# RWKV-5 recurrence with a mixer MLP behind it, one core: w and u read into all partitions by DMA, the state decayed in place, 26 zero products, and order, buffers and engines laid out anew

## The chip, the core and the metric

The kernel runs on one core of one Trainium2 chip. A core has a matmul engine (TensorE, PE in the profile, with its weight loads as PEld), three engines for elementwise work (VectorE or DVE, ScalarE or ACT, GpSimd or POOL), and SyncE (SP), which here only issues DMAs. The engines run beside each other, each through its own list of instructions in order; semaphores hold an instruction until its inputs are there. The metric is the device time of one execution in microseconds; the time of a kernel is the median of its runs.

## What is computed

Batch 4, 8 heads, 768 steps, 48 features per head. For each batch and head a 48×48 state is carried through the steps, and then a token and a channel MLP follow:

```python
for t in range(S):
    kt, vt, rt = (k[:, :, t], v[:, :, t], r[:, :, t])
    cur = np.einsum('bhd,bhe->bhde', u[None] * kt, vt)
    y[:, :, t] = np.einsum('bhd,bhde->bhe', rt, state + cur)
    state = w[None, :, :, None] * state + np.einsum('bhd,bhe->bhde', kt, vt)
...
xt = x.transpose(0, 2, 1)
h = np.maximum(xt @ w_tok1, 0.0) @ w_tok2
u = x + h.transpose(0, 2, 1)
h2 = np.maximum(u @ w_ch1, 0.0) @ w_ch2
return (u + h2)
```

x is the output of the recurrence, of shape 4×768×384. All inputs and the output are float32; the kernel's matmuls are bf16 with sums in float32.

## The kernel before

**Chunks.** The 768 steps of a batch are cut into six chunks of 128 (`C` = 6), taken in pairs. Within a chunk, k and r are scaled by powers of w (tables `wnat`, `wpair`, `wp`, and for batch 0 two tables held in `u_sb` buffers), and turned so that features lie on partitions: by TensorE transposes (`tk_ps`, `tr_ps`, `trk`) for batches 0 and 1, by DMA transposes (`rk`) for batches 2 and 3. Scores k·r go to `at_ps`, VectorE multiplies them by a mask into `AT0` and `AT1`, and the outputs are `y_ps` = AT·v plus r times the state before the chunk. The step's own term u·k·r is summed per head (`ad_ps` from the products `pr`, or `rku` reduced) and multiplied by v (`yd`, `ydb`); for batch 0 TensorE adds it to `y_ps`. The result lands in `x_b`.

**The state.** `state()` (lines 604 to 652) sums k·v into the PSUM tile `kv_ps`, of 128 partitions by 384. Chunks are grouped: two to a group in batches 0 and 1, three in batches 2 and 3 (`GB`). Within a group the sums go on in one PSUM tile, and after each chunk a bf16 copy (`S_0` or `S_1`) is kept. At the end of a group VectorE multiplies the tile by the decay of the group (`wGm`) into a bf16 tile S (line 636), and the next group begins with a product of S by the identity, which puts the state back into PSUM (lines 619 to 621). Six groups have a successor, so there are six such products of 384 columns.

**The mixer.** For each batch `mixer()` makes the token MLP (`h_ps<-x_b`, `h1r`, `hx_ps` or `hT_ps`) and the channel MLP: 24 groups of `z_ps` (three products of 384 columns each), evacuated with a relu into `zr` by ScalarE or VectorE, and the second layer `h_ps<-wch,zr`. That is most of TensorE's work, and the recurrence of the next batch is laced into it.

**The start.** w and u come as single rows of 1.5 KB on ScalarE's DMA queue (lines 360 and 365); TensorE spreads each over all partitions by a product with a row of ones (`spread`, lines 439 to 444 and 496). ScalarE takes the logarithm of the spread w into `lnw` (line 447), and every table is an Exp of `lnw` times an index. Small loads bring w and u with heads on partitions (`w_heads`, `u_heads`) for the state's decay and for `u_blk` (lines 361 to 364), turned by the tiny products `wd_ps` and `ud_ps`. SP loads r, k and v of batch 0 into `zr` rooms. Until data are there TensorE multiplies zeros: `NWARM` = 20 units, 10 of one product of 512 columns, 10 of four products of 128 (lines 1191 to 1204).

**Order.** Nothing is scheduled by rules here: `ORDER` gives the order in which tasks are emitted, and so each engine's list; `ENGINES` says for each task that may go to two engines which one has it; `BUFS` gives every tile its buffer. Each SP request has to wait for the eighth before it.

## Time and profile before

| | |
|---|---|
| Time, median of 3 runs | 161.94 us (161.71, 161.94, 162.23) |
| Span of the profiled execution, first to last instruction | 160.1 us |
| Median over that span | 1.84 us |
| HBM read, written | 20.46 MB, 4.72 MB |
| DMA requests of SP (the hardware queue) | 23.40 MB, packets of 75.4% of 16 engines' span |
| Mean granted clock of TensorE | 0.997 |

The profiled execution is one of the kernel's executions; its own time is given as the span alone, and what lies around it is known only as the difference to the median of the runs.

How to read the profile. Times are us from the start of the span. In a list of groups a row says line, engine, operation, out<-in and shape, the count, then busy time and mean duration in ns, then the idle time before these instructions and what ended most of it. Nearly all instructions carry line 279 (279 is the helper through which they are emitted), so a row is known by its tiles. In a list in order of time a row has start, duration, engine, operation and tiles; several equal instructions may be merged ("x11", with the duration of all). A row ending in [1.07 <-DMA ...] waited 1.07 us for that. In the chain that ended last the rows are pieces with start and length. Matmuls overlap each other, so their mean duration is longer than their share of TensorE; the chain gives that share.

### The profile page before, as it was taken

How to read it: one execution, taken by the hardware profiler on the slowest of the kernel's cores; microseconds unless marked ns; L12 is line 12 of the kernel's file. 1: busy time of each engine (PE TensorE's matmuls, PEld its weight loads, DVE VectorE, ACT ScalarE, POOL GpSimd, SP SyncE). 2: the span in 40 equal slices, each digit the busy share in tenths (PEclk: the TensorE clock that was granted, in tenths of full speed). 3: DMA queues.
4: the chain of work that ended last, by engine and by line, in shares of the span. 5: the costliest groups of instructions: out<-in, count | busy, mean ns of one | idle time of the engine just before them, and what ended most of it. 6: DMA issues, size and time to landing. Idle time of an engine off the chain costs nothing.

```text
span 160.1 us, 4053 instructions
## 1 busy us (share of the span) xinstructions
PE 155.0 (97%) x1617; PEld 105.7 (66%) x1618; DVE 116.0 (72%) x237; ACT 67.1 (42%) x149; POOL 79.0 (49%) x103
## 2 busy tenths in 40 slices
PE   6999999999999999999999999999999999999991
PEld 3577766777666777666667766676677666666670
DVE  4669995437866998879969988997797455445432
ACT  2859774976332465442316614234353200522100
POOL 7328899417145498434999917398972000000000
PEclk9999999999999999999999999999999999999998
DMA  5999999999998995899999999999961051620142
GB/s 129 262 261 244 218 233 190 198 208 195 229 212 151 188 197 112 186 153 201 207 231 152 236 131 250 220 216 151 196 168 53 0 123 26 197 84 17 49 147 98
DMA packets 86821, 26.90 MB, mean 168 GB/s; under 512 B 81554, under 2 KB 85908, under 8 KB 86804
## 3 DMA queue, kind: packets, MB, share of 16 engines
q1 hardware_dynamic: 84448, 23.40, 75.4%
q0 software_dynamic: 2160, 3.15, 11.5%
q8 instruction: 12, 0.20, 0.6%
q10 hardware_dynamic: 196, 0.11, 0.2%
q14 instruction: 5, 0.04, 0.1%
HBM read 20.46 MB, written 4.72 MB: 157 GB/s over the span
## 4 chain that ended last, share of the span: by engine, by line
PE 95%; DVE 1%; ACT 1%; issue 0%
PE h_ps L279 36%; PE z_ps L279 30%; PE kv_ps L279 8%; PE y_ps L279 6%; PE at_ps L279 4%; PE hT_ps L279 3%; PE hx_ps L279 3%; PE tr_ps L279 1%; PE w_ps L279 1%; PE trk L279 1%; ACT ka L279 1%; ACT rkb L279 1%; PE tk_ps L279 1%; PE u_ps L279 1%; PE ad_ps L279 0%; DVE pr L279 0%
## 5 line engine op out<-in xcount | busy, mean ns | idle before, releaser
L279 PE MATMUL h_ps<-wch,zr 128*128 128x384 bf16 (+1 forms) x300 | 55.0, 320 | 0.0
L279 PE MATMUL z_ps<-uT,wch 128*128 128x384 bf16 x288 | 52.0, 327 | 0.0
L279 ACT ACTIVATE zr<-z_ps 128x384 bf16<-128x384 f32 x52 | 23.6, 490 | 50.9 <-PE z_ps L279 50.8
L279 PEld LDWEIGHTS <-wch 128*128 128x128 bf16 x288 | 32.0, 114 | 13.9 <-DVE x_b L279 0.4
L279 PEld LDWEIGHTS <-zr 128*128 128x128 bf16 x300 | 27.0, 97 | 14.7
L279 DVE TENSOR_SCALAR zr<-z_ps 128x384 bf16<-128x384 f32 x44 | 23.1, 551 | 15.3 <-PE z_ps L279 15.2
L279 DVE TENSOR_TENSOR AT<-at_ps,mask 128x512 bf16<-128x512 f32 x36 | 23.2, 680 | 1.5 <-PE at_ps L279 1.5
L279 POOL TENSOR_TENSOR yd<-vb,adg 128x384 f32<-128x384 bf16 x15 | 12.6, 847 | 9.1 <-DVE vb L279 3.8
L279 POOL TENSOR_TENSOR ku<-kt,u_bc 128x384 f32<-128x384 f32 x11 | 11.0, 1001 | 11.9 <-DMA kt<-in_k_dram 9.8
L279 POOL TENSOR_TENSOR kr<-kt,wnat 128x384 bf16<-128x384 f32 x13 | 13.3, 1025 | 1.1 <-PE z_ps L279 1.0
L279 PEld LDWEIGHTS <-kr 128*128 128x128 bf16 (+1 forms) x196 | 11.7, 97 | 3.1 <-issue 0.4
L279 POOL TENSOR_TENSOR kr<-rt,wp 128x384 bf16<-128x384 f32 x10 | 10.6, 1069 | 3.1 <-DMA rt<-in_r_dram 3.1
L279 POOL TENSOR_TENSOR rku<-ku,rt 128x384 f32<-128x384 f32 x9 | 9.3, 1028 | 5.2 <-DVE adg L279 4.7
L279 DVE TENSOR_TENSOR u_sb<-x_b,hT_ps 128x384 bf16<-128x384 bf16 x15 | 7.7, 551 | 5.2 <-PE hT_ps L279 5.0
L279 PEld LDWEIGHTS <-wtok 128*128 128x128 bf16 x78 | 7.2, 98 | 4.9 <-issue 0.6
L279 DVE TENSOR_TENSOR osb<-u_sb,h_ps 128x384 f32<-128x384 bf16 (+1 forms) x16 | 8.3, 523 | 3.0 <-PE h_ps L279 2.7
L279 DVE TENSOR_TENSOR x_b<-y_ps,yd 128x384 bf16<-128x384 f32 x18 | 9.7, 552 | 0.7 <-PE y_ps L279 0.6
L279 PE MATMUL kv_ps<-warm 128*128 128x128 bf16 (+1 forms) x49 | 8.2, 328 | 1.4 <-DVE warm L279 1.4
L279 PE MATMUL h_ps<-x_b,wtok 128*128 128x384 bf16 x48 | 8.8, 327 | 0.0
L279 ACT CAST S<-kv_ps 48x192 bf16<-48x192 f32 x20 | 6.2, 312 | 4.9 <-PE kv_ps L279 3.7
L279 PE MATMUL y_ps<-vb,AT 128*128 128x48 bf16 (+1 forms) x240 | 8.2, 182 | 0.0
L279 PEld LDWEIGHTS <-warm 128*128 128x128 bf16 x50 | 4.5, 125 | 4.9 <-issue 3.3
(106 smaller groups left out, 202.9 us busy)
## 6 DMA issues: line engine op xcount, KB each, us to landing
out_dram<-osb SPq DMA_DIRECT2D x23, 192.0 KB, 2.2
vt<-in_v_dram SPq DMA_DIRECT2D x18, 192.0 KB, 4.2
kt<-in_k_dram SPq DMA_DIRECT2D x18, 192.0 KB, 4.9
rt<-in_r_dram SPq DMA_DIRECT2D x12, 192.0 KB, 3.4
wch<-in_moe_w_ch_dram POOLq DMA_DIRECT2D x4, 384.0 KB, 7.1
zr<-in_k_dram SPq DMA_DIRECT2D x3, 384.0 KB, 6.1
zr<-in_r_dram SPq DMA_DIRECT2D x3, 384.0 KB, 5.8
zr<-in_v_dram SPq DMA_DIRECT2D x3, 384.0 KB, 6.4
```

What stands on the lines that cost most here:

```text
L279: return lambda *args, **kw: tc.keep_in_program_order(f(*args, **kw))
```

## The change

The new kernel computes the same. What differs:

- **w and u.** SP reads the row of w into all 128 partitions of `lnw` (128 rows of 1.5 KB, 192 KB), and Ln is taken in place. The same way u goes to `u_bc`, by a later request on SP. The row loads on ScalarE's queue, the row of ones, both spreads and the copy to `u_bc` are gone. The small loads of `w_heads` and `u_heads` and the table load of ScalarE no longer wait for the row of w.
- **State.** The sums of a batch stay in one PSUM tile for all its chunks. At the end of a group VectorE multiplies the tile by `wGm` in place, and a copy to bf16 by ScalarE or VectorE gives S. The identity products are gone.
- **Zero products.** 26 units instead of 20: 14 of 512 columns and 12 of four times 128.
- **Tables of r.** A second set for groups of two exists only if a batch with DMA transposes had such groups; here none has, so only two index columns are added.
- **Order, buffers, engines.** `ORDER`, `BUFS` and `ENGINES` are new throughout.

```diff
-NWARM = 20
-WIDE_AT = [
-    0, 1, 2, 3, 4, 5, 6, 7, 8, 9,
-]
+NWARM = 26
+WIDE_AT = list(range(14))
...
-    t_wrow = once("ACT", "dma_tiny", lambda: act.dma_start(w_row, row(w).unsqueeze(0)))
+    t_wrow = once("SP", "load_w", lambda: sp.dma_start(lnw, row(w).unsqueeze(0).to_broadcast([128, dm])))
...
-    t_urow = once("ACT", "dma_tiny2", lambda: act.dma_start(u_row, row(u).unsqueeze(0)), [t_wrow])
-    t_tab = once("ACT", "act_table", lambda: act.preload_act_table_set("natural_log_exp_and_others"), [t_wrow])
-    t_ones = once("DVE", "memset_s", lambda: dve.memset(ones, 1.0))
+    t_ubc = once("SP", "load_u", lambda: sp.dma_start(u_bc, row(u).unsqueeze(0).to_broadcast([128, dm])))
+    t_tab = once("ACT", "act_table", lambda: act.preload_act_table_set("natural_log_exp_and_others"))
...
-    t_wbc = once("PE", "spread", spread("w", w_row), [t_wrow, t_ones], take=("m",))
-    t_lnw = once("ACT", "act384", lambda: act.activation(lnw, U["w"], Ln), [t_wbc, t_tab], use=[(t_wbc, "m")])
+    t_lnw = once("ACT", "act384", lambda: act.activation(lnw, lnw, Ln), [t_wrow, t_tab])
...
         def add_state():
-            if g == 0:
+            if c == 0:
                 new_bank(f"kv{plan.buf('kv')}")
...
-            if g == 0:
-                if c > 0:
-                    pe.matmul(kv[0].rearrange("p a q d -> p (a q d)"), ident,
-                              states[b, c - 1].rearrange("p a q d -> p (a q d)"),
-                              start=True, stop=False, skip_group_check=True)
             products(kv[0])
...
                 new = sb("S0", [128, HP, 2, D], bf16)
-                dve.tensor_mul(new, kv[0], wGm[G])
+                copy(on, new, kv[0])
...
         else:
-            t_state[b, c] = add("DVE", "x384p", lambda: keep_state("DVE"), [t_k, t_wGm[G]], take=(Sn,), use=okv)
+            t_r = add("DVE", "x384p", lambda: dve.tensor_mul(kv[0], kv[0], wGm[G]), [t_k, t_wGm[G]], use=okv)
+            t_state[b, c] = flex(EITHER, keep_state, [t_r], take=("S0",), use=okv)
```

**SP's list at the start of the program**, before (zr are the rooms of batch 0, vt, kt and win the loads of batch 1):

```order
L279 DMA zr<-in_k_dram 128x8x96
L279 DMA zr<-in_r_dram 128x8x96 x2
L279 DMA zr<-in_k_dram 128x8x96 x2
L279 DMA zr<-in_r_dram 128x8x96
L279 DMA zr<-in_v_dram 128x8x96 x2
L279 DMA vt<-in_v_dram 128x8x48
L279 DMA zr<-in_v_dram 128x8x96
```

and in the changed kernel:

```order
L278 DMA zr<-in_r_dram 128x8x96
L278 DMA lnw<-in_w_dram 128x384
L278 DMA zr<-in_k_dram 128x8x96
L278 DMA zr<-in_r_dram 128x8x96
L278 DMA zr<-in_k_dram 128x8x96 x2
L278 DMA zr<-in_v_dram 128x8x96
L278 DMA zr<-in_r_dram 128x8x96
L278 DMA zr<-in_v_dram 128x8x96 x2
```

The first r now stands ahead of the first k, w between them, and the last r of the batch behind the first v.

**ScalarE's list at the start**, before (wp holds the small loads, wpair and u_sb are tables, rkb and ka the evacuated transposes):

```order
L279 DMA wp<-in_w_dram 1x384
L279 DMA wp<-in_w_dram 8x2x48
L279 DMA wp<-in_u_dram 8x2x48
L279 ACT_TABLE_LOAD
L279 ACTIVATE lnw<-w_ps 128x384
L279 DMA wp<-in_u_dram 1x384
L279 ACTIVATE wpair<-lnw,iota 128x384
L279 ACTIVATE u_sb<-lnw,iota 128x384 x2
L279 ACTIVATE wpair<-lnw,iota 128x384
L279 ACTIVATE lnwd<-wd_ps 64x4 x2
L279 ACTIVATE wG_88<-lnwd 128x4
L279 COPY ka<-tk_ps 128x1024
```

and in the changed kernel:

```order
L278 DMA wp<-in_u_dram 8x2x48
L278 DMA wp<-in_w_dram 8x2x48
L278 ACT_TABLE_LOAD
L278 ACTIVATE lnwd<-wd_ps 64x4 x2
L278 ACTIVATE wG_87<-lnwd 128x4
L278 ACTIVATE lnw<-lnw 128x384
L278 ACTIVATE wpair<-lnw,iota 128x384
L278 ACTIVATE wG_88<-lnwd 128x4
L278 ACTIVATE wpair<-lnw,iota 128x384
L278 ACTIVATE u_sb<-lnw,iota 128x384 x2
L278 COPY rkb<-tr_ps 128x1024
```

The small operations on `wd_ps` moved ahead of Ln, the tables of r ahead of those of k, and r's evacuation ahead of k's.

**VectorE's list in the later half of batch 0**, before (AT are masked scores, pr the products for u, S_0 the state inside a group, S the state at its end):

```order
L279 TENSOR_TENSOR S_0_93<-kv_ps,bm 128x384
L279 TENSOR_TENSOR AT_434<-at_ps,u_sb 128x512
L279 TENSOR_TENSOR pr_488<-tr_ps,ka 128x1024
L279 TENSOR_TENSOR S_495<-kv_ps,wGm_91 128x384
L279 TENSOR_TENSOR AT_510<-at_ps,u_sb 128x512
L279 TENSOR_TENSOR AT_524<-at_ps,u_sb 128x512
L279 TENSOR_TENSOR AT_554<-at_ps,u_sb 128x512
L279 TENSOR_TENSOR AT_584<-at_ps,u_sb 128x512
L279 TENSOR_TENSOR S_632<-kv_ps,wGm_91 128x384
```

and in the changed kernel:

```order
L278 TENSOR_TENSOR AT_407<-at_ps,u_sb 128x512
L278 TENSOR_TENSOR kv_ps<-kv_ps,wGm_90 128x384
L278 TENSOR_TENSOR AT_488<-at_ps,u_sb 128x512
L278 COPY adg_512<-ad_ps 128x16
L278 TENSOR_TENSOR AT_518<-at_ps,u_sb 128x512
L278 TENSOR_TENSOR S_0_92<-kv_ps,bm 128x384
L278 TENSOR_TENSOR pr_528<-tr_ps,ka 128x1024
L278 TENSOR_TENSOR AT_551<-at_ps,u_sb 128x512
L278 TENSOR_TENSOR kv_ps<-kv_ps,wGm_90 128x384
```

The group's decay is now written back into `kv_ps`; the copies of it (`S_494` and `S_605`) stand on ScalarE's list. The first of the two decays stands earlier, ahead of the third `pr`.

More of the change, by code (lines that the diff above doesn't have):

```diff
@@ L322 @@
     krs = [const.tile([128, 2, H, P], bf16, name=f"kr{i}") for i in range(NKP)]
-    ones = const.tile([1, 128], f32, name="ones")
     u_bc = const.tile([128, dm], f32, name="u_bc")
@@ L326 @@
     NW = C // 2
[L327 to L328 removed]
+    iota_i = const.tile([128, 4 + 2 + 2 * NG + 2], i32, name="iota_i")
+    iota = const.tile([128, 4 + 2 + 2 * NG + 2], f32, name="iota")
     ident_f = const.tile([128, 128], f32, name="ident_f")
@@ L495 @@
     t_ublk = once("DVE", "u_blk", make_ublk, [t_ud, t_ub0], use=[(t_ud, "m")])
-    t_us = once("PE", "spread", spread("u", u_row), [t_urow, t_ones], take=("m",))
-    t_ubc = once("ACT", "act384", lambda: act.copy(u_bc, U["u"]), [t_us], use=[(t_us, "m")])
-    t_wp = [decay(wp, g, 6 + NG + g, [t_io, t_wbc, t_us, t_wd, t_ud, t_uw]) for g in range(NG)]
+    TABLES = sorted({GB[n // C] for n in range(B * C) if STYLE[n][0] == "dma"})
+    wps = {3: wp}
+    t_wp = {3: [decay(wp, g, 6 + NG + g, [t_io, t_wd, t_ud, t_uw]) for g in range(NG)]}
+    if 2 in TABLES:
+        wps[2] = const.tile([128, 2, dm], f32, name="wnatr")
+        t_wp[2] = [decay(wps[2], g, 6 + 2 * NG + g, [t_io]) for g in range(2)]
     loaded, asked, sent = {}, {}, {}
     t_load, i_load = {}, {}
-    def wide(b):
-        return STYLE[b * C][0] in ("f32", "win")
     def two_steps(b, c, i):
-        return STYLE[b * C][0] == "win" or i == 1 and wide(b)
+        return STYLE[b * C + c][0] == "win" or i == 1 and STYLE[b * C + c][0] == "f32"
     def load(b, c, i):
```

142 lines of the change are left out of this document (64 added, 78 removed), and 119 rows, old and new, of tables (BUFS, ENGINES, ORDER).

## The prediction

> **What bounds the kernel now.** I read the page first: the span, the busy shares, the forty slices and the shares of the chain that ended last.
>
> ```profile
> span 160.1 us, 4053 instructions
> ...
> PE 155.0 (97%) x1617; PEld 105.7 (66%) x1618; DVE 116.0 (72%) x237; ACT 67.1 (42%) x149; POOL 79.0 (49%) x103
> ...
> PE   6999999999999999999999999999999999999991
> ...
> DMA  5999999999998995899999999999961051620142
> ...
> PE 95%; DVE 1%; ACT 1%; issue 0%
> ```
>
> TensorE is full from the second slice to the last but one, and the chain lies on it for 95%. But zero products count as busy, so the next view is the busy time by stage (PE, PEld, DVE, ACT, POOL, granted clock, DMA share, GB/s).
>
> ```profile
> 12.00:25.00 13.00, 12.67 (x304) 9.27 (x302) 12.76 (x24) 10.87 (x23) 11.45 (x15) 1.00 1.20 224
> 25.00:60.00 35.00, 35.00 (x399) 25.02 (x397) 23.64 (x51) 18.46 (x42) 18.26 (x21) 1.00 1.11 198
> 60.00:100.00 40.00, 40.00 (x411) 27.22 (x410) 34.91 (x68) 16.36 (x40) 27.50 (x29) 1.00 1.08 186
> ```
>
> From 12 to 25 us VectorE works 12.76 of 13.00 us, while TensorE still fills holes with zero products: there VectorE sets the pace. From 25 us on TensorE has no hole. So a microsecond of matmuls taken out after 25 us is a microsecond off the end, if its inputs keep up; before that, what counts is when VectorE begins its masks and how many operations it has. The third view is the order of time at the start.
>
> ```profile
> 0.81 0.46 SPq L279 DMA_DIRECT2D zr<-in_k_dram  x1
> 1.33 1.74 SPq L279 DMA_DIRECT2D zr<-in_r_dram  x2
> ...
> 2.78 1.64 PE L279 MATMUL w_ps<-wp,ones 1*128 1x384 f32 x2
> ...
> 4.46 0.49 ACT L279 ACTIVATE lnw<-w_ps 128x384 f32<-128x384 f32 x1 [0.31 <-PE w_ps L279]
> ...
> 4.98 0.62 ACT L279 ACTIVATE wpair<-lnw,iota 128x384 f32<-128x384 f32 x1
> ...
> 5.51 1.10 ACT L279 ACTIVATE u_sb<-lnw,iota 128x384 f32<-128x384 f32 x2
> ...
> 6.28 0.56 DVE L279 TENSOR_TENSOR kr<-zr,wpair 128x384 bf16<-128x384 f32 x1 [1.07 <-DMA zr<-in_r_dram]
> ...
> 6.62 0.57 PE L279 MATMUL wd_ps<-ident_f,wp 8*128 8x8 f32 x2
> ...
> 7.12 2.21 PE L279 MATMUL kv_ps<-warm 128*128 128x512 bf16 x11
> ...
> 9.17 0.61 PE L279 MATMUL tk_ps<-ident,kr 128*128 128x128 bf16 x8
> ...
> 9.82 1.01 ACT L279 COPY ka<-tk_ps 128x1024 bf16<-128x1024 bf16 x1 [2.00 <-PE tk_ps L279]
> ...
> 11.95 0.69 DVE L279 TENSOR_TENSOR pr<-tr_ps,ka 128x1024 bf16<-128x1024 bf16 x1 [1.49 <-ACT rkb L279]
> ```
>
> The last row begins the stretch that VectorE fills. It waits for two evacuations on ScalarE, which wait for two groups of transposes, which stand behind the zero products.
>
> **The change: w by the load queue.** w now comes second on SP's queue, behind one load of r. The prices are the rate of the loads at the start and the quickest landing of a request into zr:
>
> ```profile
> 5.00:6.00 1.00, 1.00 (x6) 0.58 (x5) 0.21 (x2) 1.00 (x2) 0.36 (x2) 1.00 1.26 263
> ...
> DMA to landing us min/median/max: 3.9/6.2/6.4
> ```
>
> The first request, of 384 KB, lands at 0.81+3.9 = 4.7; before, the second ended VectorE's wait at 6.28, some 1.5 later, which is 384 KB at 263 GB/s. So after: r at 4.7; w, 128 rows of 1.5 KB (192 KB), 0.75 later at 5.45; k at 6.95; r of the second window at 8.4; its k at 9.9. No row shows a load that reads one row of DRAM 128 times. Bounds for its landing after issue, from these rows:
>
> ```profile
> out_dram<-osb SPq DMA_DIRECT2D x23, 192.0 KB, 2.2
> ...
> win<-in_r_dram SPq DMA_DIRECT2D x3, 384.0 KB, 8.4
> ```
>
> Issued at about 1.3, w lands between 3.5 and 9.7. I take 5.45, by the rate, since the loads around it go at that rate. The Trainium skill ("DMA: Bandwidth & Descriptors", Latency and other measured facts) reports that streams in lock step at a row pitch of 4 MiB halved the rate, 207 to 103 GB/s, with channel aliasing as the inferred cause; one row read 128 times could be like that. By it w would land at 6.2, still before the point where lateness begins to cost (below), so the sum would stay and the slow rival come nearer. No run here shows it yet.
>
> Then ScalarE: Ln 0.49 to 5.95, first table 0.62 to 6.6, a small one and the second table to 7.4, two more (1.10) to 8.5. VectorE: the two r products at 6.6 and 7.4 (0.56 each), done at 8.0; the two k products follow their tables, done at 9.1; the second window's four run to 11.1. So the r transposes are ready at 8.0 and the k transposes at 9.1.
>
> **The zero products and the added wait.** Ahead of the first transposes stand 9 wide (512) and 24 narrow (128) zero products, where it was 7 and 24 and the w spread. 3 wide and 8 narrow took 2.2 (row at 7.12), so 9 and 24 take 6.6; with the two tiny products wd and ud, 0.57 and about 0.3, TensorE comes to the r transposes at 1.39+7.5 = 8.9, after the data. Twelve narrow ones lie between them and the k transposes: at the same pace about 1.0, so k's at 10.3, done 10.75; ScalarE's copy 1.01 gives 11.75. VectorE can start its long stretch at 11.8, against 11.95: **−0.15**. Two places hide lateness: 0.9 on TensorE (8.0 to 8.9) and 0.7 to 1.2 on VectorE's products, so w may land at 6.4 for nothing, and later each microsecond costs one.
> wd is now fourth in that row instead of seventh and waits for w's small load on ScalarE's queue, issued second. Queued behind it are zero products and the r transposes, and on ScalarE the Ln. Its landing lies between 2.8 (the first small load had landed when the spread of w began) and 6.6 (wd ran). I take 3.9, 0.3 after TensorE gets there; at 6.6 the start would slip by 3.0.
>
> **In-place decay.** These rows price it; the two kv rows are pieces of the chain without and with the identity product.
>
> ```profile
> L279 PE MATMUL kv_ps<-S,ident 128*128 128x384 bf16 x6 | 2.0, 329 | 0.0
> ...
> L279 DVE TENSOR_TENSOR S<-kv_ps,wGm 128x384 bf16<-128x384 f32 x6 | 3.3, 546 | 0.0
> ...
> L279 ACT CAST x_b<-y_ps 128x384 bf16<-128x384 f32 x4 | 1.9, 478 | 1.5 <-PE y_ps L279 1.5
> ...
> L279 DVE CAST vb<-vt 128x384 bf16<-128x384 f32 x3 | 1.0, 350 | 0.0
> ...
> L279 DVE TENSOR_TENSOR kr<-rt,wp 128x384 bf16<-128x384 f32 x2 | 1.9, 931 | 0.0
> ...
> 49.27 0.17 PE kv_ps L279 x4
> ...
> 54.76 0.33 PE kv_ps L279 x5
> ```
>
> Each identity product holds the chain for 0.33−0.17 = 0.16; six fall away. Two are in the start, where VectorE sets the pace, and count there for nothing; four come after 25 us: **−0.65**. VectorE keeps six multiplications, now from PSUM into PSUM; no row has that form, so between the cheapest and dearest rows of 384 elements, 0.35 and 0.93; I take the same 0.55. What is new is a copy behind each, 0.48 on ScalarE five times and on VectorE once, before the next kv product may start. Later this is hidden by the mixer's products that stand between; if one is not hidden it costs 0.55.
>
> **Order, buffers, engines.** On VectorE the stretch from the first `pr` to the last mask of batch 0 was 11.95 to 24.03:
>
> ```profile
> 12.55 0.35 DVE L279 CAST u_blk<-ud_ps 64x4 bf16<-64x4 f32 x2
> 12.93 0.79 DVE L279 TENSOR_TENSOR kr<-zr,u_sb 128x384 bf16<-128x384 f32 x1
> ...
> 22.16 1.87 DVE L279 TENSOR_TENSOR AT<-at_ps,u_sb 128x512 bf16<-128x512 f32 x3
> 23.99 0.68 DVE L279 TENSOR_TENSOR ydb<-vb,adg 128x384 bf16<-128x384 bf16 x1
> ```
>
> u_blk and one k product leave it (0.35+0.79 = 1.14); 12 masks, 3 `pr`, three state operations and one small copy stay. From 11.8 without a hole the last mask would end at 22.75. VectorE now waits for TensorE, which waits for ScalarE's copy of the state, twice; masks stand between (1.3 us against 0.48 and a kv product), and I charge 0.5 for what they don't cover: **−1.15+0.5 = −0.65**. The u spread and u_bc's copy leave the start and hide nothing else. Three identity products of x, 3×128 columns, stand ahead of the last outputs of batch 0 now; as many columns as one identity product of the state, taken out of what follows: **−0.16**. Later 15 of the 96 z evacuations pass from VectorE to ScalarE and GpSimd loses a net nine operations of about 1 us, most of them to VectorE; none of the three comes near its stage's length, so **0**.
>
> Sum: −0.15−0.65−0.65−0.16 = −1.6. Span 160.1−1.6 = 158.5. The runs' median is 161.94, 1.84 over the profiled span; with that around it: **160.3**. Own range 159.4 to 160.9 (0.5 of uncovered waits either way and the price of w within its cover).
>
> **Rivals.**
> The DMA sets the pace (161.3 to 162.7). The DMA row is 9s to slice 29. Both new loads add 384 KB: 0.75 at 263 GB/s and about 1.0 at the later 186. The chance of being late is at the scores of batches 2 and 3:
>
> ```profile
> 82.22 2.16 SPq L279 DMA_TRANSPOSE rk<-kr  x1
> ...
> 86.99 0.62 PE L279 MATMUL at_ps<-rk 48*128 48x128 bf16 x16
> ...
> rk<-kr SPq DMA_TRANSPOSE x12, 3.9
> ...
> 96.63 1.00 POOL L279 TENSOR_TENSOR ku<-kt,u_bc 128x384 f32<-128x384 f32 x1 [4.07 <-DMA kt<-in_k_dram]
> ...
> SPq L279 <- POOL kr L279: 9.6, 7, 4.9
> ```
>
> The scores came 4.8 after the issue, with 3.9 to land: 0.9 to spare. My forecast asks for them 1.6 sooner. If loads alone set the time, the gain is lost (161.9), and 1.75−0.9 comes on top (162.7). Against it: SP waited 9.6 us for GpSimd's products, so part of the lateness was GpSimd's, which loses nine of them.
>
> w comes late (slower). Place: Ln of w on ScalarE; price: 1 us for each us after 6.4; it cancels the gain at 8.0. At the landing of the slowest load, 9.7, the end is 160.3+3.3 = 163.6. For: no load of this form in the trace; against: rate and size.
>
> Half pace at the start. The rows give the clock as 1.00, yet 3 wide and 8 narrow products (2560 columns) took 2.2, 0.86 ns a column, while 384 columns of the identity product took 0.16, 0.42 ns. If the pause at wd leaves the transposes and the 12 narrow ones at the slow pace, 16 transposes and the twelve take about 1.2 longer: 161.5. The Trainium skill ("TensorE: Matmul & The Clock Gate", Part 1: The HAM clock gate) has the array at half rate until a window of about 3.4 us was busy; the pace agrees with its half rate, the clock column does not show it.
>
> Copies on the path: if none of the six is covered, 6×0.55 = 3.3, 163.6. All start gains and no uncovered wait: 158.8.
>
> **How the numbers follow.** Forecast 0.50; better 0.08; DMA 0.16; half pace 0.08; late w 0.12; copies or another new stall 0.06. Faster means below 161.45, slower above 162.43 (0.3%, about what a measurement of this kernel can tell): faster 0.50+0.08+0.06 of the middle cases = 0.64; slower 0.12+0.06 = 0.18; the same 0.18. The range 158.9 to 162.7 leaves out the late w, the copies and a little of the better case.
>
> **What would show it.** Right: `lnw` at 5.5 to 6.2, `tr_ps` near 8.9, `pr` near 11.8, the last mask of batch 0 at 23.0 to 23.5, no `S,ident` group, TensorE without idle after 25 us. Wrong: Ln after 6.5; TensorE idle with at_ps, z_ps or kv_ps behind a DMA or S; a slower PSUM-to-PSUM multiplication.

## The result: 170.66 us, 4.3% slower, and the profile after

The changed kernel takes 170.66 us in the median (167.96 to 172.05, 4 runs) against 161.94. The ratio is 1.0428, with a 95% interval of 1.0348 to 1.0509. Here and below a ratio leaves disturbed runs out and a median doesn't, so the two need not agree to the last digit. The execution that was profiled took 170.38 us; its span is 168.7, against 160.1 before. The prediction was 160.3 in a range of 158.9 to 162.7.

The page of the changed kernel, first the span and the busy shares, then TensorE and its granted clock and the DMA in forty slices, then the shares of the chain that ended last:

```profile
span 168.7 us, 4050 instructions
...
PE 155.6 (92%) x1620; PEld 105.5 (63%) x1620; DVE 118.0 (70%) x233; ACT 74.8 (44%) x166; POOL 70.2 (42%) x94
...
PE   5799899969689999998999999989999999999992
...
PEclk9999999999959999999999999999999999999999
DMA  4999999999994049999999999999567008400033
...
PE 65%; DMA 13%; DVE 8%; issue 4%; POOL 3%; SPq 3%; ACT 1%; ACTq 0%; POOLq 0%; DVEq 0%
```

TensorE is busy for 155.6 us, nearly as before (155.0), and idle for 13.1 (168.7−155.6) where it was idle for 5.1 (160.1−155.0). So 8.0 of the 8.6 us are idle time of TensorE, 2.4 of them before 25 us and 5.6 behind. Its row of slices now has holes where there were only 9s, one slice has the clock at a half, and the chain lies on TensorE for 65% where it was 95%. The DMA row has a hole too, behind the clock's.

The stages of the changed kernel (start and end, length, then busy time of PE, PEld, DVE, ACT, POOL, granted clock, DMA share, GB/s):

```profile
25.00:36.00 11.00, 10.91 (x127) 7.63 (x126) 6.34 (x13) 7.44 (x17) 5.59 (x7) 1.00 1.08 190
36.00:50.00 14.00, 10.31 (x88) 6.89 (x86) 9.88 (x17) 7.65 (x16) 8.04 (x10) 0.90 1.06 205
50.00:60.00 10.00, 10.00 (x117) 6.84 (x115) 6.62 (x14) 5.12 (x12) 1.30 (x2) 0.97 0.26 50
...
70.00:78.00 8.00, 7.12 (x69) 4.50 (x67) 5.76 (x13) 3.81 (x9) 6.78 (x7) 1.00 1.07 201
...
110.00:122.00 12.00, 11.18 (x91) 7.59 (x89) 10.51 (x17) 7.90 (x20) 7.44 (x7) 1.00 0.94 195
```

From 25 to 122 us TensorE stands for 5.6 us (before: 0.02), and 3.69 of them lie between 36 and 50. The DMA hole lies between 50 and 60, and there TensorE has none. What happens between 36 and 50 stands in the list in order of time, cut to the instructions that matter (wch are the loads of the mixer's weights, which GpSimd issues):

```profile
26.07 0.81 POOL L278 DMA_DIRECT2D wch<-in_moe_w_ch_dram  x1
26.91 1.01 POOL L278 TENSOR_TENSOR kr<-win,wpair 128x384 bf16<-128x384 f32 x1
27.85 0.81 POOL L278 DMA_DIRECT2D wch<-in_moe_w_ch_dram  x1
...
37.99 2.63 PE L278 MATMUL z_ps<-uT,wch 128*128 128x384 bf16 x15 [1.69 <-DMA wch<-in_moe_w_ch_dram]
...
41.54 1.17 POOL L278 TENSOR_TENSOR pr<-rka,rkb 128x512 bf16<-128x512 bf16 x1 [8.78 <-ACT rka L278]
...
42.64 0.61 POOL L278 DMA_DIRECT2D wch<-in_moe_w_ch_dram  x1
...
42.96 3.32 DVE L278 TENSOR_TENSOR yd<-vb,adg 128x384 f32<-128x384 bf16 x1
...
43.27 1.96 POOL L278 TENSOR_TENSOR kr<-kt,wnat 128x384 bf16<-128x384 f32 x2
...
45.18 1.14 POOL L278 DMA_DIRECT2D wch<-in_moe_w_ch_dram  x2
46.20 1.87 DVE L278 TENSOR_TENSOR AT<-at_ps,mask 128x512 bf16<-128x512 f32 x3
...
46.93 0.95 PE L278 MATMUL z_ps<-uT,wch 128*128 128x384 bf16 x3 [2.00 <-DVE AT L278]
```

Two waits stand there. At 37.99 the products of z waited 1.69 for the second part of wch, which GpSimd issued at 27.85, behind a product `kr`. At 46.93 they waited 2.00 for VectorE's masks, and the masks stood behind one small product, `yd`. `yd` has the size of products that take 0.55 elsewhere and took 3.32 here, while GpSimd worked without a gap on `pr`, an issue, two `kr` and two issues.

The second wait has a tail. The two rows in each of the next two lists mark the start and the end of the same work on TensorE (four transposes, nine products of z, the sums for the step's own term, eight products of y). First the changed kernel:

```profile
47.67 0.63 PE L278 MATMUL trk<-ident,kr 128*128 128x128 bf16 x4
...
51.14 0.66 PE L278 MATMUL z_ps<-uT,wch 128*128 128x384 bf16 x3
```

and then a variant without that wait (`yd` on GpSimd, below):

```profile
44.98 0.40 PE L278 MATMUL trk<-ident,kr 128*128 128x128 bf16 x4
...
47.10 0.66 PE L278 MATMUL z_ps<-uT,wch 128*128 128x384 bf16 x3
```

3.47 us against 2.12: the half clock that followed the wait cost another 1.35. The account is then: 8.0 of idle time, and 0.6 more of busy time. In that 0.6 the half clock's 1.35 and the longer zero products (11.7 against 9.3, durations added up) stand against the identity products and the two spreads, which are gone (2.0 and 2.5, added up the same way).

At the start (list in order of time):

```profile
5.31 0.56 PE L278 MATMUL wd_ps<-ident_f,wp 8*128 8x8 f32 x2 [1.61 <-DMA wp<-in_w_dram]
...
6.40 0.51 ACT L278 ACTIVATE lnw<-lnw 128x384 f32<-128x384 f32 x1
...
7.72 2.60 PE L278 MATMUL kv_ps<-warm 128*128 128x128 bf16 x16
7.83 0.36 DVE L278 CAST u_blk<-ud_ps 64x4 bf16<-64x4 f32 x2 [2.27 <-PE ud_ps L278]
...
8.69 0.96 DVE L278 TENSOR_TENSOR kr<-zr,wpair 128x384 bf16<-128x384 f32 x2
...
10.15 0.61 PE L278 MATMUL tr_ps<-ident,kr 128*128 128x128 bf16 x8
...
12.96 0.69 DVE L278 TENSOR_TENSOR pr<-tr_ps,ka 128x1024 bf16<-128x1024 bf16 x1 [0.51 <-ACT ka L278]
```

VectorE reaches its long stretch at 12.96, 1.0 later than before. The mixer's first product of batch 0 begins at 24.64 instead of 23.95.

One profile doesn't fix these times. Four variants below (e15, e2, e4, e3) have the same lists up to 25 us, and in their profiles the mixer's first product comes at 25.14, 25.62, 25.80 and 25.98, later each time than in the changed kernel's. What differs is TensorE's pace ahead of `pr`: the eight transposes of r take 0.61 in the changed kernel and up to 1.06, in e3, where `pr` comes at 14.31:

```profile
10.90 1.06 PE L278 MATMUL tr_ps<-ident,kr 128*128 128x128 bf16 x8
```

The last section says what is behind that.

### The profile page after: what moved, and what is told of

Its sections match the earlier page's. It is cut to its first block, busy times and chain, and to the rows that moved or that the text cites. A ratio compares the mean times of both kernels' runs of the same rounds, so it can differ in the third digit from the quotient of the medians.

```text
span 168.7 us, 4050 instructions
## 1 busy us (share of the span) xinstructions
PE 155.6 (92%) x1620; PEld 105.5 (63%) x1620; DVE 118.0 (70%) x233; ACT 74.8 (44%) x166; POOL 70.2 (42%) x94
## 4 chain that ended last, share of the span: by engine, by line
PE 65%; DMA 13%; DVE 8%; issue 4%; POOL 3%; SPq 3%; ACT 1%; ACTq 0%; POOLq 0%; DVEq 0%
PE h_ps L278 25%; PE z_ps L278 22%; DMA wch<-in_moe_w_ch_dram 6%; PE kv_ps L278 5%; PE at_ps L278 3%; PE y_ps L278 3%; DMA rk<-kr 3%; SPq L278 3%; PE hT_ps L278 2%; DMA rt<-in_r_dram 2%; DMA wp<-in_w_dram 2%; DVE yd L278 2%; DVE zr L278 2%; DVE kr L278 1%; POOL kr L278 1%
## 5 line engine op out<-in xcount | busy, mean ns | idle before, releaser
L278 PE MATMUL h_ps<-wch,zr 128*128 128x384 bf16 (+1 forms) x300 | 52.7, 319 | 0.0
L278 ACT ACTIVATE zr<-z_ps 128x384 bf16<-128x384 f32 x67 | 30.3, 493 | 41.6 <-PE z_ps L278 41.4
L278 DVE TENSOR_SCALAR zr<-z_ps 128x384 bf16<-128x384 f32 x29 | 15.5, 552 | 15.7 <-PE z_ps L278 15.1
L278 PEld LDWEIGHTS <-kr 128*128 128x128 bf16 (+1 forms) x196 | 11.8, 98 | 4.8 <-issue 1.4
L278 POOL TENSOR_TENSOR kr<-kt,wnat 128x384 bf16<-128x384 f32 x11 | 11.3, 1031 | 7.6 <-DMA kt<-in_k_dram 5.5
L278 ACT CAST S<-kv_ps 48x192 bf16<-48x192 f32 (+1 forms) x23 | 8.0, 348 | 8.4 <-PE kv_ps L278 5.1
L278 PE MATMUL kv_ps<-warm 128*128 128x128 bf16 (+1 forms) x62 | 9.8, 315 | 1.4 <-DVE warm L278 1.4
L278 POOL TENSOR_TENSOR kr<-rt,wp 128x384 bf16<-128x384 f32 x7 | 7.7, 1106 | 7.7 <-DMA rt<-in_r_dram 7.7
L278 POOL TENSOR_TENSOR ku<-kt,u_bc 128x384 f32<-128x384 f32 x8 | 8.2, 1026 | 2.9 <-DVE rku L278 2.3
L278 PE MATMUL kv_ps<-vb,kr 128*128 128x96 bf16 (+1 forms) x100 | 7.5, 204 | 1.1 <-ACT S L278 0.6
L278 DVE TENSOR_TENSOR AT<-at_ps,u_sb 128x512 bf16<-128x512 f32 x12 | 7.9, 683 | 0.1
```

The lines of the kernel that those rows point to most:

```text
L278: return lambda *args, **kw: tc.keep_in_program_order(f(*args, **kw))
```

## The experiments

The ratios are to the kernel before, measured on the same chip.

| run | what differs | ratio (95%) | median, us |
|---|---|---|---|
| the change | | 1.0428 (1.0348 to 1.0509) | 170.66 |
| e2 | change, weight loads issued earlier by GpSimd | 1.0298 (1.0252 to 1.0344) | 167.36 |
| e3 | change, one store later on SP | 1.0512 (1.0436 to 1.0589) | 170.41 |
| e15 | change, one `yd` on GpSimd | 1.0341 (1.0271 to 1.0412) | 168.21 |
| e4 | change, these three | 1.0197 (1.0134 to 1.0260) | 165.71 |
| e1 | before, loads and in-place decay | 1.0183 (1.0109 to 1.0258) | 167.22 |
| e5 | before, in-place decay | 0.9988 (0.9942 to 1.0034) | 162.89 |
| e16 | before, in-place decay from batch 1 on | 0.9962 (0.9932 to 0.9991) | 162.11 |
| e6 | before, loads | 1.0115 (1.0047 to 1.0182) | 164.46 |
| e11 | before, loads, `wd` later | 1.0178 (1.0118 to 1.0238) | 164.81 |
| e8 | e4, start reordered | 1.0198 (1.0138 to 1.0259) | 165.96 |
| e7 | e8, w spread by TensorE | 1.0205 (1.0104 to 1.0305) | 166.79 |
| e9 | e8, nine zero products fewer | 1.0245 (1.0203 to 1.0287) | 166.10 |
| e10 | e7, nine zero products fewer | 1.0207 (1.0162 to 1.0252) | 165.33 |
| e12 | e9, a second store moved | 1.0167 (1.0119 to 1.0215) | 164.88 |
| e13 | e9, stores by ScalarE's queue | 1.0421 (1.0345 to 1.0497) | 169.32 |
| e14 | e10, stores by ScalarE's queue | 1.0346 (1.0288 to 1.0405) | 168.06 |

### The middle of the new order: e2, e3, e15, e4

The theory was that the two waits between 36 and 50 are made by GpSimd's list, in which issues stand behind products; the rival, that the DMA itself is late, because a store on SP held its queue.

**e2**, GpSimd's list:

```diff
 DMA wch_0_98<-in_moe_w_ch_dram
+DMA wch_1_99<-in_moe_w_ch_dram
 kr_67<-win,wpair
-DMA wch_1_99<-in_moe_w_ch_dram
 kr_69<-kt,wnat_81
 kr_68<-kt,wnat_81
+DMA wch_100<-in_moe_w_ch_dram x3
 pr<-rka,rkb
-DMA wch_100<-in_moe_w_ch_dram
 kr_71<-kt,wnat_81
 kr_67<-kt,wnat_81
-DMA wch_100<-in_moe_w_ch_dram x2
```

> The changed kernel with four issues of GpSimd's queue moved: the second part of the channel weights right behind the first one, and the three parts of the last weights ahead of the product pr that waits for rka. Theory: TensorE's wait of 1.7 us for wch at 38 us goes, and VectorE's yd at 43 us no longer stands beside two descriptor issues, so that part of the 2.0 us behind it goes too: 2 to 4 us less than the changed kernel's 170.7. Rival (the transfers share one bandwidth, so an earlier issue lands as late): the wait stays within 0.5 us of 1.7, and the time within 1 us of the changed kernel.

Measured: 1.0298, with an interval that ends just below that of the change (1.0344 against 1.0348). The profile of e2 in order of time:

```profile
34.17 2.63 PE L278 MATMUL z_ps<-uT,wch 128*128 128x384 bf16 x15 [1.47 <-DMA wch<-in_moe_w_ch_dram]
...
43.41 1.11 POOL L278 TENSOR_TENSOR kr<-kt,wnat 128x384 bf16<-128x384 f32 x1
43.70 1.24 DVE L278 TENSOR_TENSOR yd<-vb,adg 128x384 f32<-128x384 bf16 x1
```

The wait for masks is gone: `yd` stood beside one `kr` instead of a whole row of GpSimd's work, and took 1.24. The wait for wch is not gone but fell to the first part, 1.47 at 34.17. Nor is GpSimd's list shown to have made the 1.69 of the changed kernel: e3 and e15 below keep its order of issues, and in their profiles TensorE waits 1.04 and 0.74 for the first part and 0.20 at most for a later one. In e15:

```profile
32.69 2.63 PE L278 MATMUL z_ps<-uT,wch 128*128 128x384 bf16 x15 [0.74 <-DMA wch<-in_moe_w_ch_dram]
```

The theory holds for the second wait; for the first it isn't shown, and the rival fits better.

**e3**, SP's list:

```diff
 DMA vt<-in_v_dram x4
-DMA out_dram<-osb
 DMA rt<-in_r_dram
...
 DMA rt<-in_r_dram
-DMA out_dram<-osb
+DMA out_dram<-osb x2
 DMA_TRANSPOSE rk<-kr_68
```

> The changed kernel with one store (the first out of osb by ScalarE, for which the load queue waited 16.0 us) moved behind ten loads of batch 2. Theory: the loads of batch 2 leave from 45 us on instead of 60, the hole of the DMA engines between 50 and 60 us closes, TensorE is busy all of 70 to 78 us (it had 7.12 of 8.00), and the time falls by 0.5 to 2 us. Rival (those loads are early enough anyway, or wait for buffers): the hole stays or closes and the time stays within 0.5 us of the changed kernel.

Measured: 1.0512, nothing gained. The hole in the DMA's slices didn't close but moved to about 63 to 71 us, and TensorE's idle time from 70 to 78 fell from 0.88 to 0.33 without a gain in the time. In the change SP was held once for 16.0 us by this store; the loads behind it had that much time in hand.

```profile
SPq L278 <- ACT osb L278: 16.6, 2, 16.0
```

A queue that stands still for 16 us looks dear among SP's waits, and it cost nothing.

**e15**, the engine of one `yd`:

```diff
-ENGINES[97] = 1
+ENGINES[97] = 0
```

> The changed kernel with one step moved: the yd at 43 us by GpSimd instead of VectorE (3.32 us there). Theory (VectorE is held while GpSimd works without a gap beside it, and TensorE waits for the masks behind it): TensorE's wait of 2.0 us for AT goes, the time falls by 1.5 to 2.5 us, 0.9 to 1.5%, from the changed kernel's 170.7. Rival (the masks are late anyway): within 0.5 us of the changed kernel.

Measured: 1.0341 against 1.0428, just under the 0.9 to 1.5% of the theory, but the intervals overlap. The masks begin at 43.24 instead of 46.20; what comes next is a wait of 1.42 at 49.25, behind the late second layer's weights and ScalarE's evacuation. So the wait of 2.00 is paid back in part. The changed kernel's one run at a mean clock of 1.0 took 167.96, no more than e15's median, so some of the gain may be the clock that no longer drops.

**e4** has the three edits together.

> Both moves together, and VectorE's one yd at 43 us (3.32 us) given to GpSimd. Theory: the stalls between 36 and 78 us (3.7 and 0.9 us) go, 4 to 6 us less than the changed kernel: 164.5 to 167; what is left over the kernel before is the start (about 1.2 us later at 25 us) and the waits between 100 and 122 us. Rival (one stall hides the next): over 168.

Measured: 1.0197, far outside the interval of the change, and its span is 163.8. In the stage of the two waits TensorE is full (columns as above):

```profile
36.00:50.00 14.00, 14.00 (x151) 9.99 (x150) 9.22 (x21) 10.83 (x26) 7.49 (x8) 1.00 1.04 208
```

So, by the middles of the intervals, more than half of the 4.3% hung on the places of four weight issues in GpSimd's list and on one small product of VectorE (the store, the third edit, gained nothing alone). About 2% stay. Of the 3.7 us by which e4's span is longer than before, 1.85 are the start (the mixer's first product at 25.80 instead of 23.95, with the change's own start), and 1.9 are idle time of TensorE after 25 us, spread over four stages with at most 0.6 in each.

### The parts alone in the old order: e1, e5, e16, e6, e11

The order of before was kept and only the parts were put in, to take them apart from order, buffers and engines.

**e1** has both parts; the load of w is SP's second request, that of u stands behind the k and r loads of batch 1.

```diff
-    t_wrow = once("ACT", "dma_tiny", lambda: act.dma_start(w_row, row(w).unsqueeze(0)))
+    t_wrow = once("SP", "load_w", lambda: sp.dma_start(lnw, row(w).unsqueeze(0).to_broadcast([128, dm])))
...
-                dve.tensor_mul(new, kv[0], wGm[G])
+                dve.tensor_mul(kv[0], kv[0], wGm[G])
+                copy("ACT", new, kv[0])
```

> The kernel of before with its own order, buffers and engines, and of the change only these: w and u read into all partitions by the load queue (w as its second request, u after the loads of batch 1), no spread by TensorE, the state decayed in place with the copy on ScalarE, no identity products. The zero products stay 20. Theory (the new order of the work costs the time, the new parts do not): 159.5 to 162.5 us, that is within 1% of before, and TensorE busy without a gap after 25 us. Rival (the parts cost: w late, or the state's two steps in a row hold TensorE): 165 us or more, with TensorE waiting for the state or for w.

Measured: 1.0183, but the run is flawed by the place chosen for u. GpSimd's first `ku` waited 13.0 us for `u_bc`, and two issues of wch stood behind it:

```profile
44.93 0.99 POOL L279 TENSOR_TENSOR ku<-kt,u_bc 128x384 f32<-128x384 f32 x1 [13.00 <-DMA u_bc<-in_u_dram]
45.88 1.14 POOL L279 DMA_DIRECT2D wch<-in_moe_w_ch_dram  x2
```

It shows nothing of the parts, but that a waiting product on GpSimd holds the weights: TensorE waited 3.56 for wch at 51.87. The parts were then run one by one, with the load of u earlier.

**e5**, the decay alone (the last three lines of the diff above, the identity products out, one PSUM tile for a batch).

> The kernel of before with its order, buffers and engines; of the change only the state decayed in place in its bank (VectorE multiplies, ScalarE copies to the bf16 tile) and no identity products of the state. Theory (the parts as they were priced): the four identity products after 25 us go, 0.65 us, and between 12 and 25 us the product of the next step waits up to 0.5 us twice for the two steps: within 0.5% of before. Rival (the two steps in a row cost each batch): over 1% slower, with TensorE's kv_ps waiting for ScalarE's S after 25 us too.

Measured: 0.9988 (0.9942 to 1.0034), no difference. In the one execution that was profiled (164.18 us, above the median) a `kr` of VectorE beside GpSimd's took 3.03, and TensorE waited 1.47 for it:

```profile
26.79 2.91 POOL L279 TENSOR_TENSOR kr<-win,wpair 128x384 bf16<-128x384 f32 x3
...
28.04 3.03 DVE L279 TENSOR_TENSOR kr<-win,wpair 128x384 bf16<-128x384 f32 x1
...
31.13 0.40 PE L279 MATMUL tr_ps<-ident,kr 128*128 128x128 bf16 x4 [1.47 <-DVE kr L279]
```

Whether the other executions have this wait isn't known. **e16** leaves batch 0 with its two identity products, so that the start stays as it was, and has the decay in place from batch 1 on:

```diff
-                dve.tensor_mul(new, kv[0], wGm[G])
+                if b == 0:
+                    dve.tensor_mul(new, kv[0], wGm[G])
+                else:
+                    dve.tensor_mul(kv[0], kv[0], wGm[G])
+                    act.copy(new, kv[0])
```

> The kernel of before with its order, buffers and engines; the state is decayed in place from batch 1 on (copy on ScalarE), batch 0 stays as before. Theory (TensorE sets the end after 25 us and loses four identity products of 0.16): 0.4 to 0.7 us less than before, 0.2 to 0.4%. Rival (the state's two steps, one behind the other, make the next product wait): same as before or slower, with TensorE waiting for ScalarE's S.

Measured: 0.9962 (0.9932 to 0.9991), which is 0.6 us on 162 (0.15 to 1.1 by the interval), where four identity products at 0.16 make 0.64. Who waited for the copies stands in the view of the state's tile:

```profile
L279 DVE TENSOR_TENSOR kv_ps<-kv_ps,wGm x4: 555/555/556, 51.9 to 114.6; 128x384 f32<-128x384 f32 x4
...
  PE kv_ps L279: 0.2, 1
```

TensorE waited for one copy, 0.2 us. This is the only version that is faster than the kernel before, and it takes 4.5% less than the changed kernel (0.9962/1.0428).

**e6**, the loads alone (the first two lines of e1's diff, the same for u, both spreads out).

> The kernel of before with its order, buffers and engines; of the change only the loads: w into all partitions as the load queue's second request, u by the same queue behind the third k block of batch 1 (earlier than in the run e1, where GpSimd waited 13 us for it), no spread by TensorE. Theory: 192 KB ahead of batch 0's blocks put every later block back, VectorE's first product starts 1 to 1.3 us later than 6.28, and 0.8 to 1.6 us of it reach the end: 0.5 to 1.0% slower than before. Rival (as forecast: w lands in time and costs nothing): within 0.3% of before.

Measured: 1.0115 (1.0047 to 1.0182). The loads in the place of the spreads cost 1.2% by themselves.

```profile
6.00 0.52 ACT L279 ACTIVATE lnw<-lnw 128x384 f32<-128x384 f32 x1 [1.61 <-DMA lnw<-in_w_dram]
...
7.71 0.56 DVE L279 TENSOR_TENSOR kr<-zr,wpair 128x384 bf16<-128x384 f32 x1 [2.50 <-ACT u_sb L279]
```

Ln begins at 6.00, where it began at 4.46, and VectorE's first product at 7.71 instead of 6.28. TensorE also waited 2.42 for w's small load, and in this profile its clock was at a half from about 7.5 to 10.9. To see whether that pause is the cause, **e11** puts `wd`, and on ScalarE `lnwd` and wG, behind eleven more zero products:

```diff
-wd_ps<-ident_f,wp
 kv_ps<-warm x11
+wd_ps<-ident_f,wp
```

> e6 (only the loads of w and u changed, old order) with TensorE's small product wd moved behind the eleven zero products that follow it, so that no zero product waits for the small load of w. Theory (what the loads cost in e6 is TensorE's idle 2.4 us ahead of wd, which kept it at half its pace until 11 us): the transposes of k take 0.6 us instead of 1.06 and start before 9.0 instead of 9.29, pr before 12.2 instead of 12.77, and the time comes to within 0.4% of before. Rival (192 KB ahead of the blocks set the start): VectorE's first product stays at 7.7 and pr at 12.5 to 12.9, and the time within 0.4% of e6's 1.0115 times before.

Measured: 1.0178 (1.0118 to 1.0238), no gain. The wait for `wd` is gone, and Ln begins at 5.54, but VectorE's first product and `pr` (12.56) come hardly earlier, as the rival had it, since the r block behind the 192 KB of w is late now:

```profile
7.58 0.56 DVE L279 TENSOR_TENSOR kr<-zr,wpair 128x384 bf16<-128x384 f32 x1 [2.37 <-DMA zr<-in_r_dram]
```

So in these two runs w's load costs twice, by its own landing and by what it pushes back. The clock was at a half in e11 too, a little later (10.4 to 13.8 us), so e11 doesn't tell what half pace costs there. Nor do e6's runs tell: three with a mean clock of 0.999 or 1.0 took 164.23 to 164.91, three with 0.979 to 0.99 took 163.81 to 165.04, but that mean counts as full what lies ahead of the first entry of the clock record (last section). What share of the 1.2 and 1.8% is the clock's stays open.

### The start in the new order: e8, e7, e9, e10

**e8** takes e4 and moves Ln and the four tables ahead of `lnwd` and wG on ScalarE, and `u_blk` behind six products on VectorE (six in the list, where the expectation says four):

```diff
 ACT_TABLE_LOAD
+lnw<-lnw
+wpair<-lnw,iota x2
+u_sb<-lnw,iota x2
 lnwd<-wd_ps x2
...
-u_blk<-ud_ps x2
...
 kr_69<-zr,wpair x2
+u_blk<-ud_ps x2
 kr_70<-zr,u_sb x2
```

> The kernel of e4 with the start put in another order: ScalarE takes the logarithm of w and the four tables ahead of the small logarithm and its two exponentials, and VectorE evacuates ud behind four of its eight products instead of ahead of them. Theory: VectorE's first product starts at 7.2 to 7.6 us instead of 8.69, and 1.0 to 1.5 us of it reach the end: 0.6 to 0.9% less than e4. Rival (the blocks land too late for it): within 0.4 us of e4.

Measured: 1.0198, as e4. The r products come at 7.31 instead of 8.69, but the transposes not before 10.56: they stand behind sixteen narrow zero products, which took 3.08 us.

```profile
7.64 3.08 PE L278 MATMUL kv_ps<-warm 128*128 128x128 bf16 x16
...
10.56 0.61 PE L278 MATMUL tr_ps<-ident,kr 128*128 128x128 bf16 x8
```

**e7** is e8 with w as a row on ScalarE's queue, spread by TensorE, as before.

> As e8, but w is read as one row by ScalarE's queue and spread over the partitions by one product of TensorE, as before the change; u stays with the load queue. Theory: without 192 KB ahead of them the blocks of batch 0 land about 1 us earlier, 0.7 to 1.3 us less than e8. Rival (the start is paced by VectorE, not by the loads): within 0.4 us of e8.

Measured: 1.0205 (1.0104 to 1.0305). Ln comes at 5.31 and the r products at 6.48, and the transposes at 10.76, behind the same zero products. Nothing gained.

**e9** and **e10** leave out nine of the zero products ahead of the transposes, in e8 and in e7:

```diff
-        t = add("PE", "warm", keep_warm(512 if i in WIDE_AT else 128), [t_warm])
+        t = add("PE", "warm", (lambda: None) if i in LEFT_OUT else keep_warm(512 if i in WIDE_AT else 128), [t_warm])
```

> e8 without nine of the 26 zero products: six of the seven between ud and the first transposes of r (sixteen matmuls took 3.08 us there in e8) and the three between these and the transposes of k (twelve matmuls, 0.83 us). Theory: TensorE is what starts late; the products of r are there at 8.4 us, but the transposes stand behind the zero products until 10.56. They start at 8.4 to 9.0, VectorE's first pr at 12.0 to 12.6 instead of 13.37 (its own eight products end at 12.29), and 0.7 to 1.3 us less than e8 in all. Rival (TensorE then works at half its pace until it has been busy for longer, as before the transposes in e8): pr not before 13.0, and within 0.4 us of e8.

> e7 (w as one row, spread by TensorE) without the same nine zero products. Theory: the blocks of batch 0 are no longer behind 192 KB of w, so VectorE's products end about 1 us earlier than in e9 and pr starts at 11.0 to 11.8: 0.6 to 1.2 us less than e9, within 1% of before. Rival (the load of w costs nothing beside the order of the start): within 0.4 us of e9.

Measured: 1.0245 and 1.0207. In e9 the transposes come at 7.98 and the mixer's first product at 23.62, which is 0.3 earlier than before and 1.0 to 2.4 earlier than in the five profiles with the change's start (24.64 to 25.98). By the ratios none of it reaches the end:

```profile
74.02 0.48 ACT L279 COPY osb<-h_ps 128x384 f32<-128x384 f32 x1 [3.69 <-DMA out_dram<-osb]
...
74.55 2.60 PE L279 MATMUL z_ps<-uT,wch 128*128 128x384 bf16 x15 [1.47 <-ACT osb L279]
```

ScalarE waits for a store to leave its buffer, and the products of z wait for ScalarE. In e10 the products of z wait 1.2 for the turned `uT` and 0.6 for wch instead. The three pairs that differ by the spread alone (e7 and e8, e10 and e9, e14 and e13) differ by 0.1% to 0.75%, with intervals that overlap. In the last two the spread is ahead, and the 0.75% of e14 is the size of its theory; but what w's load costs in the new order stays open.

### What is left: e12, e13, e14

**e12** takes e9 and moves that store ahead of the transposing load of `uT` on SP:

```diff
 DMA_TRANSPOSE rk<-kr_72
+DMA out_dram<-osb
 DMA_TRANSPOSE uT<-u_sb
-DMA out_dram<-osb
```

> e9 with one more store moved: that of the first osb by VectorE, ahead of the transposing load of uT instead of behind it. In e9 ScalarE's next copy into that buffer waited for it until 74.02 (3.7 us idle) and TensorE 1.5 us for that copy. Theory (the gain of the start is given back at places where a queue holds a step in its order): that wait goes, TensorE is busy 7.5 or more of the 8.0 us from 70 to 78, 1 to 2 us less than e9. Rival (the transfers are late as such, and the next wait takes its place): within 0.5 us of e9.

Measured: 1.0167 (1.0119 to 1.0215) against 1.0245 (1.0203 to 1.0287) for e9: 1.3 us, as the theory had it, but the intervals overlap. The wait at 74 us is gone (from 70 to 78 TensorE is busy for 8.00), and, as the rival had it, another stands ten microseconds earlier, of the same kind, on VectorE, where it was 0.60 in e9:

```profile
64.70 0.56 DVE L279 COPY osb<-h_ps 128x384 f32<-128x384 f32 x1 [3.07 <-DMA out_dram<-osb]
...
66.21 0.33 PE L279 MATMUL kv_ps<-vb,kr 128*128 128x96 bf16 x4 [1.70 <-DVE vb L279]
```

**e13** and **e14** (on e9 and e10, without e3's edit) send three stores by ScalarE's queue, right behind the copies, so that SP's loads can't hold them:

```diff
+                    q = "ACT" if (b, sg, si) in [(0, 0, 0), (0, 0, 2), (0, 1, 1)] else STORE[b]
```

> The changed kernel with the weights issued early and yd on GpSimd (as in e4), the start and the nine fewer zero products of e9, and the three stores of batch 0 that follow a copy by ScalarE issued by ScalarE's own queue right behind the copy, so that they stand in no other queue and their buffers come free at once; no store is moved in the load queue. Theory (the rest is the waits for output buffers): VectorE's and ScalarE's waits for stores to land (6.2 us of VectorE's time in e12) fall under 1 us, TensorE's idle time between 60 and 78 us under 0.5 us, and the time comes to 1.004 to 1.010 times before. Rival (many small waits): 1.014 to 1.02 times before, with a wait of another name in their place.

> e13 with w read as one row and spread by TensorE, as before the change. Theory of the loads: as in the old order (e6: 1.0115), 0.5 to 1.2% less than e13. Rival (in the new order another wait takes up what the start gains, as in e7 and e10): within 0.3% of e13.

Measured: 1.0421 and 1.0346; e13's theory fell, and the range of its rival with it. ScalarE itself is now held, since each request waits for the eighth before it, and the load of u is still in flight: u, issued at 52.49, landed at 56.28, and the store, whose copy had ended at 53.87, was issued at 56.36:

```profile
56.36 0.38 ACTq L279 DMA_DIRECT2D out_dram<-osb  x1
56.78 0.51 ACT L279 CAST vb<-vt 128x384 bf16<-128x384 f32 x1 [2.91 <-DMA u_bc<-in_u_dram]
...
57.34 0.33 PE L279 MATMUL kv_ps<-vb,kr 128*128 128x96 bf16 x4 [2.04 <-ACT vb L279]
```

A store that waits on SP holds loads; on ScalarE it holds `vb`, and TensorE with it.

The last 1.7 to 2% have no single cause. In e4 and e8 about half of it is the start; where the start was made shorter (e9, e10, e12 to e14), a wait of TensorE of 1.2 to 2.0 us stood between 50 and 78 us, behind another engine from edit to edit. No run undid the new buffers alone, so whether they or the order make these waits stays open.

## Why the prediction was wrong

**The step that failed** is the last one of the sum, "Order, buffers, engines", where "none of the three comes near its stage's length", so it was put at 0. It counted the work that passes from engine to engine and held it against the stage. What costs is the place in a list: one `yd` of VectorE beside a full GpSimd, which took 3.32 instead of 0.55 and held TensorE for 2.00, and products ahead of weight issues on GpSimd. VectorE was busy for 9.88 of 14 us in that stage, so by work alone there was room. e4 puts the price of these places at 2.3% (at least 0.9% by the intervals); the rest, some 1.7 to 2%, lies in the start and in later places of the same lists or in their buffers, and that part of the cause stays open.

**w by the load queue.** Forecast: landing at 5.45, with 6.4 "for nothing". Measured: Ln at 6.40 in the changed kernel, at the bound of the cover, where ScalarE also did `lnwd` and wG first; from issue to landing 4.7 us, so 6.0. That landing is inside the bounds, and near the 6.2 that the prediction worked out for aliased rows. In the old order e6 and e11 price the loads at 1.2 and 1.8%, where the r and k blocks behind them come late as well. Whether the cover held in the new order stays open.

**The zero products and the added wait.** Forecast for tr, tk and `pr`: 8.9, 10.3, 11.8; measured: 10.15, 11.27, 12.96. The zero products ahead of tr took 6.4 where 6.6 was taken, so the term that was mis-sized is the wait of `wd`: 1.61 where 0.3 was taken (it ran at 5.31, between the bounds of 2.8 and 6.6), and that is the 1.25 by which tr came late. What the prediction left out is `u_blk` on VectorE: it stands ahead of the r products and waits 2.27 for `ud`, which stands on TensorE behind `wd` and nine zero products. So VectorE's first product came at 8.69, where 6.6 was forecast; but in e8, where it came at 7.31, tr still came at 10.56, behind the zero products. The rival of half pace did come about: in e3, with the same start, it reached the transposes, and `pr` came 1.35 later than in the changed kernel's profile, where the rival had 1.2. Yet by e9 the start alone doesn't set the end: 1.0 us or more won there brought nothing.

**In-place decay.** Right in mechanism and size. The multiplication from PSUM into PSUM took 0.557 on the mean where 0.55 was taken, in the changed kernel:

```profile
L278 DVE TENSOR_TENSOR kv_ps<-kv_ps,wGm 128x384 f32<-128x384 f32 x6 | 3.3, 557 | 0.6 <-PE kv_ps L278 0.6
```

and e16, which has it from batch 1 on, gains 0.6 (0.15 to 1.1) against 0.65. e5, which has all six, shows no gain within its interval; why is open.

**VectorE's stretch.** Forecast: shorter by 0.65. Measured: from 12.96 to the end of the last masks at 25.28, 12.3 against 12.1 before; the 1.14 that left it turned into holes (1.31 idle against 0.24), 0.65 and 0.56 of them before the two operations that wait for TensorE's sums in `kv_ps`.

**The rivals.** The DMA as the bound: no; the hole of its slices cost nothing (e3). Whether the wait for wch is an issue that came late isn't shown (e2, e3, e15). Late w: in part, as above. Half pace: seen at the start, as above. The one that came true is "copies or another new stall", which had 0.06; its sign, TensorE idle with `z_ps` behind a DMA, is there at 37.99, but the larger wait stands behind a mask, which the prediction didn't name, and the dearest price of any rival, 163.6, is far from 170.66. With two lists changed throughout, it should have been looked for at every place where an issue or a mask stands behind something that waits.

## What to carry to other kernels

Where engines run through fixed lists, price the places and not the work: for each instruction that may wait, ask what stands behind it on its engine, DMA issues above all, and who waits for that. A gain at the start can be swallowed by later waits, as in e9, so follow each gain to the end. And when several edits come at once, put each one alone into the old order: here that found the one part worth keeping (e16).

## What the runs showed of the hardware

- **VectorE held by GpSimd.** A product of VectorE with both inputs in SBUF took 3.32 (`yd`, the changed kernel) and 3.03 (`kr`, e5) instead of 0.55 while GpSimd worked without a gap, and 1.24 beside one `kr` of GpSimd (e2). In e2 and e5 it ended 0.42 after GpSimd's last product did; the `yd` of the changed kernel ended 1.05 after it, and two DMA issues of GpSimd followed that product. The Trainium skill ("SBUF — State Buffer", Who interferes with whom) says that such an instruction contends with a GpSimd instruction that reads SBUF, and that the port pair they share is an exclusive lock. The traces agree, and show that it lasts through several GpSimd instructions in a row, not one.
- **The clock behind a wait.** After 2.00 us without a matmul the granted clock of the changed kernel was at a half from 47.14 to 50.55 us. The clock record of the traces shows when that happens. From its first entry on it goes in steps of 3.41 us, in every run here. A step in which TensorE stood for 1.84 us or more (thirteen such steps, in eleven runs) was followed by a step at half, one with 1.81 or less by a step at full, with one exception (1.46 at the start of e11, and half). So it counts where a wait falls: that of the changed kernel lay inside one step (43.73 to 47.14). That of e3, 1.99, was cut by a step's end at 46.28 into 0.55 and 1.44, and its clock stayed at 1.00. The changed kernel's run with a mean clock of 1.0 took 167.96, those with 0.986 to 0.99 took 170.38 to 172.05; in e3 it is 169.74 and 169.81 against 171.01 and 171.60. The Trainium skill ("TensorE: Matmul & The Clock Gate", Part 1: The HAM clock gate) puts the drop behind an idle window of about 3.4 us; here 1.84 of idle time within a step was enough, and the length of the half clock, 3.41 (in e6 and e11 too), agrees with its window.
- **Half pace at the start, with the column at 1.00.** The clock record has its first entry at 9.10 us before, and at 9.59, 10.06, 11.47, 11.03 and 12.15 in the changed kernel, e15, e2, e4 and e3; the column counts what lies ahead of it as full. The matmuls there ran at about half pace: in e3 eight transposes took 1.06 at 10.90, and 0.61 at 12.62; in e8, with the first entry at 10.51, sixteen narrow zero products took 3.08 from 7.64 on, and twelve took 0.83 from 11.01 on. The later the first entry, the later, by and large, the mixer's first product: 24.64, 25.14, 25.62, 25.80 and 25.98 in the five kernels with the change's start.
- **One row into all partitions.** The load of w, 192 KB from one row of 1.5 KB, took 4.7 us from issue to landing. The stores of 192 KB take 2.2, but the other loads of that size, rt, vt and kt, take 3.7, 4.2 and 4.4 in the changed kernel, so w's is not far from them.
